# The attention's instructions ordered by a written table, with four queries loaded early and normalisations on two engines

## The chip, the cores and the metric

The kernel runs on one core of a Trainium2 chip. A core has five engines that work side by side, each in the order of its own instruction list: TensorE (PE in the profile; matmuls), VectorE (DVE), ScalarE (ACT), GpSimd (POOL) and SyncE (SP, which here only starts transfers). They wait for each other through semaphores. The metric is the device time of one execution in microseconds (us).

## The reference

A block-summary attention feeds two feed-forward layers of the same form. Each query sees the keys less than 16 positions away and one summary per block of 32 keys (the maximum of the keys, the mean of the values):

```python
k_sum = k.reshape(B, H, nb, block, D).max(axis=3)      # B 2, H 8, S 768, D 64, block 32
v_sum = v.reshape(B, H, nb, block, D).mean(axis=3)
scores_l = scale * q @ k.T                             # kept where |i - j| < 16
scores_s = scale * einsum(q, k_sum) + log(block)
a = softmax(concat(scores_l, scores_s))
x = a @ concat(v, v_sum)                               # 1536 tokens, 512 wide
x = leaky_relu(x @ moe_w_in, 0.01) @ moe_w_out         # 512 -> 2048 -> 512
x = mish(x @ moe2_w_in) @ moe2_w_out
```

The feed-forward weights arrive as 64-bit floats.

## The kernel before

**Groups.** The attention works on 24 groups, each 256 tokens of one batch for one pair of heads; four groups with the same tokens make x for these tokens. A group's steps are: its query transfer (`load_q`, into one of four tiles `qt`, so group g needs that group g-4 has been scored) and its values' transfer (`load_vw`); the key window, copied by GpSimd in two halves (`k_window`, L257: the keys, then the block sums); the scores on TensorE (`scores`, L367); the maximum on VectorE (`score_max`, L381); four exponentials on ScalarE (`score_exp`, L391); the reciprocal of the sum on VectorE (`score_inv`, L400 and L401); the normalisation, one multiplication 128 x 480, on GpSimd (`score_norm`, L406); the transposition on TensorE (`p_transpose`, L412); its evacuation to `pT` on ScalarE or VectorE (`p_evac`, L420 and L422); the product with the values on TensorE (`av`, L431); and x in two parts, the high one as fp32r on ScalarE or VectorE and what is left on VectorE (`x_part`, L446 to L450). Groups 0 to 3 go singly, the others in pairs. Block sums of keys (`k_sum`, L298) and values (`sum_vs`, L340) are made by VectorE, those of the first batch's values by TensorE (`sum_v0`, L317), with an evacuation into the value tiles (`place_v0`, L327 and L329).

**Feed-forward blocks.** A matmul in 32 bits is made of three products of high and low parts. Each step of layer 1 is an up of 12 matmuls per block of tokens (`up`, L465), the activation in two parts (`leaky_a` on ScalarE, L476 and L477; `leaky_b` on VectorE, L481) and a down of 12 matmuls (`down`, L520), which follows three blocks later. Ups and downs are issued in halves of six. Fifteen of them run between the attention's steps; the first six have 256 columns, all others 512.

**Weights.** A weight tile goes through: a transfer into one of three `raw` buffers, the scaling of its top half on ScalarE (`w_scale`, L130), the merge on VectorE (`w_merge`, L137), the high part (`w_hi`, L166 or L164) and the low part on GpSimd (`w_lo`, L173). The tiles of the second part of the weights stand in memory that the attention uses, and can be written once its last step is over.

**Order.** Everything until the attention's end is written as steps with estimated durations, needs, buffers and a turn (partly from the table `RATE`, L64). A planner, `run_order()`, picks the steps one by one on a model of the engines and so sets the order of each engine, of the transfers on SP, and the engine of a step that has two. Where the model finds TensorE idle early on, it puts in matmuls on an idle tile (`warm`, L220). The chosen steps are then issued under a manual schedule. Behind the attention the order is that of the loop over the remaining blocks.

Of the kernel before, what the change touches and what calls it, by code (L numbers as in the profile page):

```python
# [28 lines left out]
def kernel(  # L29
# [182 lines left out]
    def warm(n, w=128):  # L212

        if not idle:
            idle["t"] = ap1.tile([P, 128], F32, name="idle")
            nc.vector.memset(idle["t"], 0.0)
            idle["p"] = bank("h0")
        t = idle["t"]
        for _ in range(n):
            nc.tensor.matmul(idle["p"][:, 0:w], t, t[:, 0:w], start=True, stop=True)  # L220
# [131 lines left out]
    st = {}  # L352

# [71 lines left out]
    def av(g):  # L425

        px, t = st[g]
        w = vw[groups[g][2]]
        for n in range(NB):
            for s in range(2):  # L430
                nc.tensor.matmul(  # L431
                    px[s * D:(s + 1) * D, n * QB:(n + 1) * QB],
                    w[:, n, s, :],
                    t[:, s * (NB // 2) + n // 2, (n % 2) * QB:(n % 2 + 1) * QB],
                    start=True, stop=True,
                )
        st[g] = px
# [137 lines left out]
    if True:  # L575
# [30 lines left out]
        batches = [[g] for g in range(4)] + [[g, g + 1] for g in range(4, NG, 2)]  # L606
        first_score = {g: u for gs, u in zip(batches, (-4, -4, -4, -4) + RATE) for g in gs}
# [4 lines left out]
        steps = []  # L612

        class Step:
            pass

        def step(on, fn, needs=(), turn=0.0, take=(), give=(), tag=None):
            x = Step()
            x.on, x.fn, x.turn, x.take, x.give, x.tag = on, fn, turn, take, give, tag
            x.needs = [(d, 0.07) if isinstance(d, Step) else d for d in needs]  # L620
            x.end = None
            steps.append(x)
            return x

        store = {
            "bank": ["a0", "a1", "y0", "y1", "y2", "y3"], "h": ["h", "h"], "raw": [0] * 3, "top": [0] * 2,
            "mid": [0] * 4, "q": [], "kw": [0] * 4, "s": [0] * 4, "pT": [0] * NPT, "g": [0] * (LAG + 1), "t": [0] * 2,
        }
        held = {}
        closed = [False]  # L630

        def load(fn, mb, needs=(), turn=0.0, take=(), give=()):
            return step({"SP": mb}, fn, needs, turn, take, give)

        def later(f, *a):
            return lambda eng: f(*a)

        def given(x, end):
            x.end = end
            return x  # L640


        landed = [4.1, 5.4, 7.7, 9.0]
        K = {(0, h): given(step({}, None), landed[h]) for h in range(4)}
        Q = {g: given(step({}, None), landed[g] + 0.2) for g in range(4)}
        W_LOAD, W_TOP, W_MERGE, W_HI, W_LO = {}, {}, {}, {}, {}

        def need_slot(i):
            return i if i < 2 * nA else 100

        for i in range(2 * nA):
            u = need_slot(i)
            W_LOAD[i] = load(later(w_load), 0.524, [], max(u - 7, -4.1) if i else -5, [("raw", ("raw", i))])
        for i in range(2 * nA, 2 * nA + 7):
            W_LOAD[i] = load(later(w_load), 0.524, [], 8 + i - 2 * nA, [("raw", ("raw", i))])
# [14 lines left out]
        for h in range(3):  # L670
            PLACE[0, 3].needs.append((PLACE[0, h], -0.4))
# [366 lines left out]
```

## Time and profile before

| what | us |
|---|---|
| time of three runs, median (lowest, highest) | 603.07 (602.11, 603.58) |
| the profiled execution's own time | 602.08 |
| its span, first to last instruction | 599.9 |
| TensorE busy in the span | 589.8 |
| VectorE busy | 384.5 |
| ScalarE busy | 313.9 |
| GpSimd busy | 193.9 |

The time is taken outside the profile; the span is that of the instructions in one profiled execution, and its own time has some 2.2 us around the span. A busy share is a mean over stages of different kind. In the slices of the page TensorE is at 9 tenths or more from the second slice of 15 us to the last but one, and the granted clock of TensorE is 0.999 of full speed over the span.

### The profile page before, as it was taken

To read this page: it belongs to the slowest core of one execution; us is meant where nothing else is said; L and a number is where in the kernel's file an instruction comes from. 1 tells how busy PE (TensorE), PEld (TensorE's weight loads), DVE (VectorE), ACT (ScalarE), POOL (GpSimd) and SP (SyncE) were. 2 spreads that over 40 slices of the span, in tenths; PEclk is the share of its full clock that TensorE was granted. 3 is DMA by queue.
4 is the path that set the end of the run, shared out by engine and by line. 5 is a ranking of instruction groups with operands and counts; after the bars stand their busy time and mean duration, and the time that the engine had idled before them with its cause. 6 is when DMAs were issued, how large, how long until landed. Compare 5 with 4: busy or idle time off the path is not lost.

```text
span 599.9 us, 9152 instructions
## 1 busy us (share of the span) xinstructions
PE 589.8 (98%) x3334; PEld 480.1 (80%) x3334; DVE 384.5 (64%) x777; ACT 313.9 (52%) x671; POOL 193.9 (32%) x214
## 2 busy tenths in 40 slices
PE   8899999999999999999999999999999999999997
PEld 7688878787888888888888888888888888888885
DVE  7799776356451114114445988776799998678684
ACT  5878866357662223225646655454467555444442
POOL 7666742164430001004430323332332232232221
PEclk9999999999999999999999999999999999999999
DMA  9997453026741000001537210000012000001011
GB/s 322 344 311 238 159 167 124 2 87 219 256 140 37 0 2 0 1 0 71 172 109 245 72 35 1 0 1 0 2 70 72 0 1 1 1 35 37 0 72 70
DMA packets 19373, 52.10 MB, mean 87 GB/s; under 512 B 2176, under 2 KB 5248, under 8 KB 19072
## 3 DMA queue, kind: packets, MB, share of 16 engines
q1 hardware_dynamic: 18752, 51.00, 25.6%
q8 instruction: 26, 0.43, 0.3%
q10 hardware_dynamic: 576, 0.52, 0.3%
q14 instruction: 19, 0.16, 0.1%
HBM read 48.37 MB, written 3.15 MB: 86 GB/s over the span
## 4 chain that ended last, share of the span: by engine, by line
PE 94%; DVE 2%; ACT 2%; DMA 1%; POOL 1%; issue 0%; SPq 0%; DVEq 0%; ACTq 0%
PE h L465 43%; PE y L520 22%; PE y L527 21%; PE a L431 2%; PE a L367 2%; PE a L412 1%; PE y L541 1%; DMA kT<-in_kT_dram 1%; DMA raw<-in_moe_w_out_dram 1%; ACT top L130 0%; POOL w L173 0%; DVE s L381 0%; DVE ks L298 0%; DVE mid L137 0%; PE y L317 0%
## 5 line engine op out<-in xcount | busy, mean ns | idle before, releaser
L465 PE MATMUL h<-x,w 128*128 128x512 f32 (+1 forms) x1188 | 288.4, 388 | 0.3 <-ACT g L477 0.2
L465 PEld LDWEIGHTS h<-x,w 128*128 128x128 f32 x1188 | 217.6, 188 | 49.9 <-ACT g L477 0.6
L520 PE MATMUL y<-g,w 128*128 128x512 f32 (+1 forms) x612 | 145.8, 384 | 0.4 <-POOL w L173 0.4
L527 PE MATMUL y<-w,g 128*128 128x512 f32 x552 | 136.9, 394 | 0.0
L194 POOL TENSOR_TENSOR g<-e,g 128x512 fp32r<-128x512 f32 x47 | 73.5, 1565 | 186.7 <-ACT g L191 172.6
L520 PEld LDWEIGHTS y<-g,w 128*128 128x128 f32 x612 | 110.1, 188 | 24.9 <-POOL w L173 0.6
L527 PEld LDWEIGHTS y<-w,g 128*128 128x128 f32 x552 | 103.7, 188 | 24.1
L173 POOL TENSOR_TENSOR w<-mid,w 128x512 fp32r<-128x512 f32 x45 | 63.1, 1410 | 114.4 <-ACT w L166 111.2
L481 DVE TENSOR_TENSOR g<-t,g 128x512 fp32r<-128x512 f32 (+1 forms) x51 | 35.6, 702 | 88.8 <-ACT g L477 88.6
L476 ACT ACTIVATE t<-h 128x512 f32<-128x512 f32 (+1 forms) x51 | 28.9, 567 | 87.1 <-PE h L465 87.1
L137 DVE SCALAR_TENSOR_TENSOR mid<-raw,top 128x512 int32<-128x512 int32 x64 | 56.7, 894 | 26.6 <-POOL w L173 15.1
L130 ACT ACTIVATE top<-raw 128x512 f16<-128x512 bf16 x64 | 50.2, 797 | 26.5 <-DMA raw<-in_moe_w_out_dram 8.9
L492 ACT ACTIVATE e<-h 128x512 f32<-128x512 f32 x48 | 28.7, 598 | 67.6 <-PE h L465 60.0
L503 DVE SCALAR_TENSOR_TENSOR u<-u,r 128x512 f32<-128x512 f32 x48 | 37.1, 773 | 25.8 <-ACT r L496 25.5
L495 ACT ACTIVATE r<-u,two 128x512 f32<-128x512 f32 x48 | 34.8, 724 | 31.0 <-DVE u L494 31.0
L391 ACT ACTIVATE s<-s,nm 128x120 f32<-128x120 f32 x96 | 36.5, 382 | 14.8 <-DVE nm L381 14.6
L166 ACT CAST w<-mid 128x512 fp32r<-128x512 f32 x62 | 37.7, 617 | 11.5 <-DVE mid L137 6.8
L191 ACT CAST g<-e 128x512 fp32r<-128x512 f32 x48 | 29.5, 615 | 20.6 <-DVE e L505 20.5
L494 DVE SCALAR_TENSOR_TENSOR u<-e 128x512 f32<-128x512 f32 x48 | 34.6, 720 | 1.1
L406 POOL TENSOR_TENSOR s<-s,r 128x480 f32<-128x480 f32 x24 | 24.7, 1032 | 30.1 <-DVE r L401 25.8
L504 DVE SCALAR_TENSOR_TENSOR u<-u,r 128x512 f32<-128x512 f32 x48 | 33.2, 691 | 1.4
L505 DVE SCALAR_TENSOR_TENSOR e<-e,u 128x512 f32<-128x512 f32 x48 | 33.1, 689 | 1.1
(71 smaller groups left out, 432.9 us busy)
## 6 DMA issues: line engine op xcount, KB each, us to landing
raw<-in_moe_w_in_dram SPq DMA_DIRECT2D x32, 512.0 KB, 4.3
raw<-in_moe_w_out_dram SPq DMA_DIRECT2D x32, 512.0 KB, 3.8
vw<-in_vW_dram SPq DMA_DIRECT2D x24, 192.0 KB, 5.2
kT<-in_kT_dram SPq DMA_DIRECT2D x8, 400.0 KB, 7.3
out_dram<-yp SPq DMA_DIRECT2D x12, 256.0 KB, 2.0
q<-in_qT_dram SPq DMA_DIRECT2D x20, 128.0 KB, 7.1
vS<-in_vS_dram SPq DMA_DIRECT2D x2, 1024.0 KB, 8.8
v<-in_v_dram SPq DMA_DIRECT2D x2, 768.0 KB, 7.9
```

What stands on the lines that cost most here:

```text
L130: (tc.keep_in_program_order if pin else id)(nc.scalar.mul(out=do, in_=di, mul=4.0))
L137: nc.vector.scalar_tensor_tensor(out=d, in0=wraw.pop(i)[:, 0:2 * DM].rearrange("p (f w) -> p f w", w=2)[:, :, 1], scalar=13, in1=wtop.pop( ...
L166: nc.scalar.copy(out=w[:, 0], in_=wmid[i])
L173: (eng or nc.gpsimd).tensor_sub(out=w[:, 1], in0=wmid.pop(i), in1=w[:, 0].bitcast(F32))
L194: (nc.vector if lo == "dve" else nc.gpsimd).tensor_sub(out=dst_lo, in0=src, in1=dst_hi.bitcast(F32))
L391: nc.scalar.activation(out=s[:, n], in_=s[:, n], func=AF.Exp, scale=-1.0, bias=nm[:, n:n + 1], accum_out=sm[:, n:n + 1],)
L465: nc.tensor.matmul(ph[:, 0:n], w[:, a, kt * P:(kt + 1) * P], x[:, c, kt, o:o + n], start=(kt == 0 and i == 0), stop=(kt == KT - 1 and i == 2),
L481: nc.vector.tensor_sub(out=g[:, 1, 0:n], in0=t[:, 0:n], in1=g[:, 0, 0:n].bitcast(F32))
L495: nc.scalar.activation(out=r, in_=u, func=AF.Ln, bias=two[:, 0:1])
L503: V.scalar_tensor_tensor(out=u, in0=u, scalar=2.0, in1=r, op0=ALU.add, op1=ALU.mult)
L520: mm = nc.tensor.matmul(y[d][:, o:o + n], w[:, a, d * P:(d + 1) * P], g[:, c, 0:n], start=sta and not second, stop=sto,)
L527: nc.tensor.matmul(y[d], g[:, a, d * P:(d + 1) * P], w[:, c], start=sta, stop=sto,)
```

## The change

The planner, its steps, `RATE` and the estimates go. In their place stands `ORDER`, a text of words, each one step: a letter for the kind, the group's or block's number, a letter for the engine where there is a choice (a, d, p for ScalarE, VectorE, GpSimd) and, behind a colon, the PSUM banks. V, v, w, q, k, r are transfers (first batch's values, windows of values, weights, queries, second batch's keys and values); K and J key sums; C and D the two parts of a key window; S, M, E, I, N, T, P, A the group's steps from scores to the product with the values; X and L the parts of x; t, m, h, l the steps of a weight; s, p the value sums of the first batch and their placement, R, Z those of the second; U, O halves of an up or a down; G, g the two parts of its activation; d the evacuation of y; warm the idle matmuls. The words are issued one after another.

Three things besides are new. The queries of groups 4 to 7 go to a tile of their own, `early`, in the memory that x's second block takes later. `score_norm` has an engine: 11 of the 24 normalisations are VectorE's, 13 GpSimd's. `leaky_b` has one as well: 12 of the first 15 blocks' subtractions are GpSimd's, six of 256 columns and six of 512. By the letters some more steps change their engine: three evacuations of `pT` and four high parts of x go from VectorE to ScalarE, three high parts of weights, two low parts and one placement to VectorE. There are 29 idle matmuls instead of 23.

```diff
-    RATE = (-1.0, -0.5, 3.5, 4.0, 6.5, 7.0, 7.0, 9.5, 10.5, 13.0)
+    ORDER = """
+        V.0 K.0 C.0 v.1 D.0 w.0 K.1 C.1 S.0:a0,a1 V.1 D.1 M.0 warm.1 S.1:y0,y1 q.5 E.0 C.2 q.6 M.1 w.1 E.1 C.3 I.0
+        v.0 K.2 C.4 N.0d C.5 I.1 warm.11 T.0:a0 D.4 v.3 K.3 D.2 N.1p S.2:a1,y0 q.4 P.0a D.3 M.2 C.6 S.3:y1,y2 E.2
...
+    """
...
+    SINGLE = 4
...
+    early = xp.tile([P, 2 * KT * TB], F32, tag="x1", name="early")
+    qe = [early[:, i * GT:(i + 1) * GT].rearrange("p (t n) -> p t n", n=NB) for i in range(4)]
+
     def load_q(g, eng):
         b, c, hp = groups[g]
-        t = qt[g % len(qt)]
+        t = qe[g - 4] if 4 <= g < 8 else qt[g % len(qt)]
...
-    def score_norm(g):
+    def score_norm(g, eng):
         s, r = st[g]
-        nc.gpsimd.tensor_mul(out=s, in0=s, in1=r.unsqueeze(2).to_broadcast([P, NB, WN]))
+        ENG[eng].tensor_mul(out=s, in0=s, in1=r.unsqueeze(2).to_broadcast([P, NB, WN]))
...
-    def leaky_b(t, g, n):
-        nc.vector.tensor_sub(out=g[:, 1, 0:n], in0=t[:, 0:n], in1=g[:, 0, 0:n].bitcast(F32))
+    def leaky_b(t, g, n, eng=None):
+        (eng or nc.vector).tensor_sub(out=g[:, 1, 0:n], in0=t[:, 0:n], in1=g[:, 0, 0:n].bitcast(F32))
         return g
...
+        def step(name, fn, *a):
+            run[name] = lambda eng, banks: fn(*a, *([eng] if eng else []), *([banks] if banks else []))
...
+            for word in ORDER.split():
+                name, _, banks = word.partition(":")
+                eng = engines.get(name[-1])
+                name = name.rstrip("adp") if eng else name
+                if name.startswith("warm"):
+                    warm(int(name[5:]))
+                else:
+                    run[name](eng, banks.split(",") if banks else None)
```

What the table does to the lists is shown at three places. The first is GpSimd's list at the start, before, from the second half of group 1's window to the second normalisation (`kw<-kT` is a copy of keys, `kw<-ks` of block sums, `s<-s,r` a normalisation):

```order
L257 TENSOR_SCALAR kw<-ks 128x4x24
L257 TENSOR_SCALAR kw<-kT_110 128x4x64
L257 TENSOR_SCALAR kw<-kT_110 128x4x32
L257 TENSOR_SCALAR kw<-kT_110 128x4x64
L257 TENSOR_SCALAR kw<-kT_110 128x4x32
L257 TENSOR_SCALAR kw<-ks 128x4x24
L406 TENSOR_TENSOR s<-s,r 128x480
L257 TENSOR_SCALAR kw<-ks 128x4x24
L406 TENSOR_TENSOR s<-s,r 128x480
```

The same stretch in the changed kernel, whose lines are 30 to 31 higher:

```order
L287 TENSOR_SCALAR kw<-ks 128x4x24
L287 TENSOR_SCALAR kw<-kT_111 128x4x64
L287 TENSOR_SCALAR kw<-kT_111 128x4x32
L287 TENSOR_SCALAR kw<-kT_111 128x4x64
L287 TENSOR_SCALAR kw<-kT_111 128x4x32
L287 TENSOR_SCALAR kw<-kT_111 128x4x64
L287 TENSOR_SCALAR kw<-kT_111 128x4x32
L287 TENSOR_SCALAR kw<-kT_111 128x4x64
L287 TENSOR_SCALAR kw<-kT_111 128x4x32
L287 TENSOR_SCALAR kw<-ks 128x4x24 x2
L437 TENSOR_TENSOR s<-s,r 128x480
L287 TENSOR_SCALAR kw<-ks 128x4x24
```

Two further groups' key windows and one more pair of block sums now stand ahead of the second normalisation, and the first one has left this list.

The second place is VectorE's list from the reciprocal of group 2 on, before (`mid<-raw,top` is a weight's merge, `vw<-y` a placement, `pT<-y` an evacuation, `x` the first high part):

```order
L400 TENSOR_SCALAR r<-sm 128x4
L401 RECIPROCAL r<-r 128x4
L137 SCALAR_TENSOR_TENSOR mid<-raw,top_86 128x512
L400 TENSOR_SCALAR r<-sm 128x4
L401 RECIPROCAL r<-r 128x4
L327 COPY vw_99<-y_309 24x512
L422 COPY pT<-y_366 120x512
L450 CAST x_401<-a_269 128x256
```

The changed kernel from the same reciprocal on:

```order
L431 TENSOR_SCALAR r<-sm 128x4
L432 RECIPROCAL r<-r 128x4
L437 TENSOR_TENSOR s<-s,r 128x480
L164 SCALAR_TENSOR_TENSOR mid<-raw,top_86 128x512
L191 CAST w<-mid 128x512
L357 COPY vw_100<-a_324 24x512
L431 TENSOR_SCALAR r<-sm 128x4
L432 RECIPROCAL r<-r 128x4
L357 COPY vw_101<-a_324 24x512
L453 COPY pT<-y_374 120x512
L164 SCALAR_TENSOR_TENSOR mid<-raw,top_87 128x512
```

The normalisation of group 2 and the high part of the first weight are now in this list, two placements instead of one, and the reciprocal of group 3 stands between them.

The third is TensorE's list around the last product with the values (`a<-pT,vw`), before; `h<-x,w` is an up, `y<-g,w` a down:

```order
L412 MATMUL a_1893<-ident,s 120x128 x4
L465 MATMUL h<-x_1012,w 128x512 x6
L465 MATMUL h<-x_1606,w 128x512 x5
L520 MATMUL y_1666<-g,w 128x512
L431 MATMUL a_1878<-pT,vw_100 64x64 x8
L431 MATMUL a_1893<-pT,vw_101 64x64 x8
L465 MATMUL h<-x_1606,w 128x512 x6
L520 MATMUL y_1666<-g,w 128x512 x2
```

The changed kernel:

```order
L443 MATMUL a_1898<-ident,s 120x128 x4
L496 MATMUL h<-x_1054,w 128x512 x6
L496 MATMUL h<-x_1649,w 128x512 x4
L462 MATMUL a_1893<-pT,vw_100 64x64 x8
L462 MATMUL a_1898<-pT,vw_101 64x64 x8
L496 MATMUL h<-x_1649,w 128x512 x6
L551 MATMUL y_1547<-g,w 128x512
```

In all, 282 matmuls of 512 columns (two of 256 counted as one) stand ahead of the last product, where it was 271; the downs behind it are taken in thinner slices. The next up that waits before, the 12 matmuls at 145.61 below, stands 89 such matmuls behind the product, and 86 in the changed kernel.

## Rows read from the trace of the kernel before

**Rows 1.** Busy time by stretch: us from:to, length, PE, PEld, DVE, ACT, POOL, clock, DMA, GB/s

```profile
0.00:40.00 40.00, 33.76 (x468) 29.09 (x472) 31.64 (x118) 28.36 (x96) 27.64 (x69) 1.00 0.99 327
29.00:52.00 23.00, 21.38 (x279) 19.63 (x279) 21.29 (x71) 17.90 (x64) 15.09 (x25) 1.00 1.00 305
40.00:500.00 460.00, 459.74 (x2459) 372.82 (x2452) 279.44 (x546) 243.91 (x509) 140.46 (x130) 1.00 0.24 78
```

**Rows 2.** Timeline of TensorE, first 45 us: start, us, instruction, count, idle before

```profile
7.59 2.50 PE L220 MATMUL h<-idle 128*128 128x128 f32 x20
10.14 0.75 PE L367 MATMUL y<-kw,q 64*64 64x120 f32 x16
...
21.44 0.50 PE L367 MATMUL a<-kw,q 64*64 64x120 f32 x4 [0.41 <-DMA q<-in_qT_dram]
...
30.81 1.15 PE L431 MATMUL a<-pT,vw 120*64 120x64 f32 x32 [1.11 <-DVE pT L422]
...
40.34 1.70 PE L520 MATMUL y<-g,w 128*128 128x256 f32 x12
```

**Rows 3.** Timeline of GpSimd, first 45 us

```profile
8.62 0.67 POOL L257 TENSOR_SCALAR kw<-kT 128x256 f32<-128x256 f32 x2 [0.69 <-DMA kT<-in_kT_dram]
9.81 0.27 POOL L257 TENSOR_SCALAR kw<-ks 128x96 f32<-128x96 f32 x1 [0.53 <-DVE ks L298]
10.05 0.99 POOL L406 TENSOR_TENSOR s<-s,r 128x480 f32<-128x480 f32 x1
...
13.94 1.27 POOL L406 TENSOR_TENSOR s<-s,r 128x480 f32<-128x480 f32 x1
...
35.74 1.28 POOL L173 TENSOR_TENSOR w<-mid,w 128x512 fp32r<-128x512 f32 x1 [1.42 <-ACT w L166]
```

**Rows 4.** Timeline of ScalarE, first 45 us

```profile
13.00 0.38 ACT L391 ACTIVATE s<-s,nm 128x120 f32<-128x120 f32 x1
...
15.62 0.57 ACT L329 COPY vw<-y 24x512 f32<-24x512 f32 x1
...
23.78 0.39 ACT L391 ACTIVATE s<-s,nm 128x120 f32<-128x120 f32 x1
...
30.05 0.56 ACT L420 COPY pT<-a 120x512 f32<-120x512 f32 x1
```

**Rows 5.** Timeline of VectorE, first 45 us

```profile
13.71 0.66 DVE L137 SCALAR_TENSOR_TENSOR mid<-raw,top 128x512 int32<-128x512 int32 x1
...
16.23 0.69 DVE L327 COPY vw<-y 24x512 f32<-24x512 f32 x1 [0.77 <-ACT vw L329]
```

**Rows 6.** ScalarE's groups by line and shape, 0 to 60 us: busy, mean ns, idle

```profile
L130 ACT ACTIVATE top<-raw 128x512 f16<-128x512 bf16 x11 | 8.7, 795 | 2.7 <-DMA raw<-in_moe_w_in_dram 2.1 <-DMA raw<-in_moe_w_out_dram 0.5
L166 ACT CAST w<-mid 128x512 fp32r<-128x512 f32 x7 | 4.4, 628 | 0.8 <-DVE mid L137 0.8
L420 ACT COPY pT<-a 120x512 f32<-120x512 f32 x6 | 3.3, 581 | 1.3 <-PE a L412 1.3
...
L448 ACT CAST x<-a 128x256 fp32r<-128x256 f32 x4 | 1.5, 373 | 0.2 <-PE a L431 0.2
```

**Rows 7.** VectorE's groups by line and shape, the whole span

```profile
L340 DVE TENSOR_REDUCE vs<-vS 128x16 f32<-128x512 f32 x8 | 8.4, 1050 | 0.0
L298 DVE TENSOR_REDUCE ks<-kT 128x24 f32<-128x768 f32 x8 | 7.5, 938 | 0.9 <-DMA kT<-in_kT_dram 0.9
L422 DVE COPY pT<-a 120x512 f32<-120x512 f32 x11 | 7.4, 687 | 6.2 <-PE a L412 6.1
...
L164 DVE CAST w<-mid 128x512 fp32r<-128x512 f32 x2 | 0.8, 411 | 0.0
```

**Rows 8.** Timeline of TensorE and VectorE at the attention's end

```profile
123.35 1.15 PE L431 MATMUL a<-pT,vw 120*64 120x64 f32 x32
...
145.61 3.07 PE L465 MATMUL h<-x,w 128*128 128x512 f32 x12 [0.17 <-ACT g L477]
...
127.16 5.18 DVE L137 SCALAR_TENSOR_TENSOR mid<-raw,top 128x512 int32<-128x512 int32 x3 [1.19 <-POOL w L173]
```

More of the change, by code (lines that the diff above doesn't have):

```diff
@@ L219, in warm @@
         for _ in range(n):
[L220 removed]
+            nc.tensor.matmul(idle["p"][:, 0:P], t, t, start=True, stop=True)
     def build_const():
@@ L423, in p_evac, with av @@
         st[g] = (pp, t)
[L425 to L437, printed above, removed]
+    def av(gs):
+        for g in gs:
+            px, t = st[g]
+            w = vw[groups[g][2]]
+            for n in range(NB):
+                for s in range(2):
+                    nc.tensor.matmul(
+                        px[s * D:(s + 1) * D, n * QB:(n + 1) * QB],
+                        w[:, n, s, :],
+                        t[:, s * (NB // 2) + n // 2, (n % 2) * QB:(n % 2 + 1) * QB],
+                        start=True, stop=True,
+                    )
+            st[g] = px
     def x_part(g, c, eng):
@@ L605 @@
         NI = len(items)
-        batches = [[g] for g in range(4)] + [[g, g + 1] for g in range(4, NG, 2)]
-        first_score = {g: u for gs, u in zip(batches, (-4, -4, -4, -4) + RATE) for g in gs}
+        batches = [[g] for g in range(SINGLE)] + [[g, g + 1] for g in range(SINGLE, NG, 2)]
         X = 15
[L612 to L640, printed above, removed]
@@ L643 @@
[L643 to L655, printed above, removed]
@@ new lines @@
+        run = {}
+        def step(name, fn, *a):
+            run[name] = lambda eng, banks: fn(*a, *([eng] if eng else []), *([banks] if banks else []))
+        for i in range(2 * nA + 7):
+            step(f"w.{i}", w_load)
+        for i in range(2 * nA + 4):
+            step(f"t.{i}", w_scale)
+            step(f"m.{i}", w_merge, False)
+            step(f"h.{i}", w_hi)
+            step(f"l.{i}", lambda eng: w_lo(ENG[eng]))
+        for i in range(2):
+            step(f"V.{i}", load_v0, i, SP)
+            step(f"s.{i}", sum_v0, i)
+            step(f"r.{i}", load_vs, i, SP)
+            for q in range(4):
+                step(f"R.{4 * i + q}", sum_vs, i, q)
@@ new lines @@
+        for h in range(4):
+            step(f"K.{h}", k_sum, 0, h)
+            step(f"k.{h}", load_k, 1, h, SP)
+            step(f"J.{h}", k_sum, 1, h)
+            step(f"p.{h}", place_v0, h)
+            step(f"Z.{h}", place_vs, h)
+        for g in range(NG):
+            step(f"q.{g}", load_q, g, SP)
+            step(f"v.{g}", load_vw, g, SP)
+            step(f"C.{g}", k_window, g, 0)
+            step(f"D.{g}", k_window, g, 1)
+            step(f"M.{g}", score_max, g)
+            step(f"E.{g}", score_exp, g)
+            step(f"I.{g}", score_inv, g)
+            step(f"N.{g}", score_norm, g)
+            step(f"T.{g}", p_transpose, g)
+            step(f"P.{g}", p_evac, g)
+            step(f"X.{g}", x_part, g, 0)
+            step(f"L.{g}", x_part, g, 1, None)
@@ new lines, with up_half, act_a, act_b @@
+        for gs in batches:
+            step(f"S.{gs[0]}", scores, gs)
+            step(f"A.{gs[0]}", av, gs)
+        def up_half(n, half):
+            _, _, _, j, o, N, _, sidx, _ = slots[n]
+            if half == 0:
+                gq[n] = up_begin(n)
+            up(sidx, j, o, N, gq[n], half)
+        def act_a(n):
+            gq[n] = leaky_a(gq[n], slots[n][5])
+        def act_b(n, eng):
+            gq[n] = leaky_b(*gq[n], slots[n][5], ENG[eng])
+        def down_half(m, half):
+            nonlocal cur_y
+            _, layer, _, _, o, N, i, sidx, last = slots[m]
+            if i == 0 and o == 0 and half == 0:
+                cur_y = new_y()
+            down(sidx, layer, i == 0, last, o, N, gq[m], cur_y, half)
+            if half == 1:
+                gq.pop(m)
@@ new lines, in drain_half @@
+        def drain_half(j, eng):
+            drain(0, 0, j, 0, TB, cur_y, eng)
+        for n in range(X):
+            step(f"G.{n}", act_a, n)
+            step(f"g.{n}", act_b, n)
+            for half in range(2):
+                step(f"U.{2 * n + half}", up_half, n, half)
+                step(f"O.{2 * n + half}", down_half, n, half)
+        for j in range(2):
+            step(f"d.{2 * j}", drain_half, j, "act")
+            step(f"d.{2 * j + 1}", drain_half, j, "dve")
+        engines = {"a": "act", "d": "dve", "p": "pool"}
```

295 lines of the change are left out of this document (30 added, 265 removed).

## The prediction, made before the changed kernel was run

> **What bounds the kernel now.** I read the busy time by stretches first, then TensorE's timeline where the stretches show gaps, then the other engines' timelines at those gaps. From 40 to 500 us TensorE is busy 459.74 of 460.00 [rows 1]: no order of the same matmuls gains there. In the first 40 us it is busy 33.76, so 6.25 are idle, and some of the busy time is filler: 46 records of .125 each, the first 20 of them 2.50 [rows 2], 5.75 us. So 12 us at the start is all that an order can win, and it is won only if the chain that feeds TensorE gets shorter: a group's scores, maximum, exponentials, normalisation, transposition, evacuation and product with the values. Here the other engines are the limit: VectorE is busy 21.29 of 23.00 from 29 to 52 us [rows 1]. So the question is how far TensorE's useful work is ahead at 40 us, and whether the lead lasts to the end.
>
> Words below: S, M, E, I, N, T, P, A of a group are those eight steps in turn (I is the reciprocal); X and L are the high and low part of its x; C and D the two halves of a key window; t, m, h, l the four steps of a weight (scaling, merge, high part, low part); U and O half an up or a down of a block.
>
> **The start, to the placement of the value sums.** The letters for engines and the new order work together here. Up to 9.29, when GpSimd has copied the second key window (8.62 + .67, [rows 3]), both kernels do the same. Before, GpSimd goes on to group 2's window sums at 9.81 (.27), and TensorE scores group 2 at 10.14 [rows 2, 3]. In the changed kernel GpSimd copies groups 4 and 5 first (C.4, C.5: 2 x .67) and two sums (D.4, D.2: 2 x .27): 9.29 + 1.34 + .54 = 11.17, so S.2 at 11.2, 1.05 later. What covers this is that ScalarE and GpSimd lose other work from the chain: N.0 and N.2 go to VectorE, and the scaling of the first weight comes behind E.2 instead of ahead of it. From S.2 to the end of E.2 it was 10.14 to 13.00, 2.86 [rows 2, 4]; so E.2 ends at 14.06. Then P.1 .58, t.0 .80 [rows 6], m.0 .68 (.66 in [rows 5], and a handoff), h.0 .41 on VectorE [rows 7]: 16.55 with the handoffs, where the first placement can begin; before it began at 15.62 [rows 4].
>
> N on VectorE is in no row. Its bounds: 480 of 512 columns of the .66 of an undisturbed merge [rows 5], .62, and the 1.73 that a merge took beside GpSimd's subtractions (5.18 for three, [rows 8]). I take .65, since GpSimd at the start mostly copies; at the upper end it is the third rival. Low parts of g on GpSimd aren't there either: half of a 512-wide subtraction's 1.28 [rows 3], .64, up to a normalisation's .99. I take .66. VectorE takes over 11 N, 7.2 us, and gives up 12 of 51 low parts of g (six of 256 columns, six of 512: at N's .65 for 480 columns, 6.2) and three P (2.1); the rest that changes hands is a few high parts either way. Its sum is the same within 2 us; what changes is when it works.
>
> **The placements and the first up.** Four placements run one after another in both kernels, VectorE's .69, ScalarE's .57 [rows 4, 5]: 2 x .69 + 2 x .57 + handoffs = 2.65, so 19.2. Behind them, each waiting for the one before or standing behind it in ScalarE's row, P.2 on VectorE .69, m.1 .68, h.1 .63, P.3 .58, A.3 .69 (16 matmuls, from the timeline's 32 in 1.15, [rows 2], and the drain), X.3 .37 [rows 6, 7]: 3.64, and with the handoffs E.4 begins at 23.0. Before it began at 23.78 [rows 4]. This is the **early queries'** share: before, S.4 waited .41 for its query until 21.44 [rows 2], since each of the four query tiles is free only when group g-4 has been scored. Four more queries in x's memory need no such wait; S.4 then hangs on its windows and banks, which are there by 20. The gain is not .41 but what E.4 can use, .8 with the shorter work ahead of it on ScalarE. The four loads cost SP nothing new (20 + 0 before, 16 + 4 now), but they stand ahead of two weight loads; no weight is wanted so early that this shows (the second is scaled at about 17).
>
> **From E.4 to 40 us.** E.4 to E.7 are back to back on ScalarE, 23.78 to 30.05 [rows 4], 6.27, and will be again: 29.27. I.7 .4 and P.5 .69 [rows 7], then A.4 at 30.5; before 30.81 [rows 2]. The up behind it waits for GpSimd, which has N.7 .99 and a low part 1.28 [rows 3] ahead: 32.2, against 31.9 before. VectorE's two value sums (1.05 each, [rows 7]), P.7 and the scores of 8 bring A.6 to 33.7 and S.8 to 36.3; key sum J.3 .94 [rows 7], a merge and L.7 bring the second half of up 3 to 37.55, and 4 ups in all are done at 39.1 with half an up more; two downs then end at 40.55. Before, at 40.34, TensorE has done U.0 to U.7, O.0, O.1 and the same scores [rows 2]. The changed kernel at 40.55 has U.8 too, which is worth .77 (half of 12 matmuls of 256, 1.70 less the overlap, [rows 2]). **Lead: .77 - .21 = .6 us.**
>
> **From 40 us on.** The two lists of TensorE hold the same matmuls, and TensorE in both is full as long as every operand is early enough. In the changed order VectorE is back to back from 29 to 52, and hands A.8 its operand at 52.0 to 52.35 when TensorE is about to ask at the same time; I put it at nothing, the margin being some tenths. The attention's end moves: the last A stands 11 matmuls of 512 columns later in TensorE's work. Behind it the weights of the next part start (their memory is the attention's), and before, TensorE ran from 123.35 to 145.44 on work that didn't need them, then waited .17 [rows 8]. Less A's own 1.08 that is 89 matmuls of .236 average; now it is 86, 21.4 us of cover instead of 22.1. If the weight chain keeps its 22.26, the stall is .87, .7 more. But drains and merges stand earlier in the new order, so the chain may shorten by as much. Bounds: -.17 (stall gone) to +.7; I take 0, since in the new order the drains of y stand behind two merges of that chain on VectorE, where four stood ahead of them, and the chain's last wait before was ScalarE's g behind a weight's scaling, which the order now sets otherwise.
>
> **The sum.** The profiled execution took 602.08 (span 599.92 and 2.16 around it); the median of the three runs shown is 603.07, .99 above. The forecast goes on the median: 603.07 - .6 = **602.5**, and by bounds of the end alone 601.7 to 603.2. The handoffs, some thirty of .05 to .1, make it 601.3 to 603.7.
>
> **Rivals.**
> *No lead, 603.1.* Two engines in each other's way: GpSimd's normalisation beside a merge on VectorE took 1.27 at 13.94 and .99 alone at 10.05 [rows 3, 5]. If N.0 on VectorE and C.5 on GpSimd can't run together, C.5, D.2, S.2 and all behind start .63 later, and the .6 is gone. For: that row. Against: GpSimd's row there is a normalisation with two inputs, and the window copies at the start, with one, show no such lengthening (.67 beside VectorE's key sums). The Trainium skill, "SBUF — State Buffer", section "Who interferes with whom", says that a VectorE instruction with two SBUF inputs contends with a GpSimd instruction that reads SBUF, and that whoever issues first holds the shared pair for the whole instruction while the other is fully blocked; by it N.0 holds C.5 up for all of its .65, which speaks against this change. The trace agrees in part: a full block would have cost that normalisation .43 (from 13.94 to the merge's end at 14.37), and it lost .28.
>
> *More lead, 600.8.* By my dates TensorE still has gaps of 3.4 us between 20 and 40 us (the largest before U.4, .95, and before S.8, .65). Several hang on handoffs that I put too long or on an engine's order that leaves room. If half closes, 1.7 more. For: the early queries let every later score be moved freely. Against: VectorE's list has no free place in it.
>
> *Slower, 605.6: VectorE is the bound from 29 to 52 us.* It has in the changed order hardly a pause there (before, 1.71 of 23 us [rows 1]). If the three merges m.3 to m.5 meet GpSimd's low parts of g and take 1.73 each [rows 8] instead of .68, everything behind on VectorE is 3.15 later, A.8 with it, and TensorE waits. The price decides from 2.4 us: .6 of lead and 1.8 to be seen. For: low parts on GpSimd, eleven N on VectorE, both inputs of each in the memory they share. Against: at 13.71 [rows 5] it was GpSimd that lost time and the merge took .66.
>
> **How the numbers follow.** Chances: forecast .45, more lead .25, no lead .13, slower .17. A measurement of this kernel tells some 0.3% from no change, 1.8 us: faster is under 601.3, slower above 604.9. The faster case lies below 601.3 with .22 of its .25, the forecast's own lower edge adds .08: faster .30. Slower: .15 of the third rival and .01 of the forecast's upper edge, .16. The same: .54. The range has to take in most of more lead and the lower part of slower: 600.2 to 604.9 leaves out about .07 below and .13 above.
>
> **What would show it.** In the changed profile: S.2 on TensorE at 11.2 and E.4 on ScalarE at 23.0 (start right); A.4 at 30.5 and two downs ended at 40.55 with half an up more (lead right); N on VectorE at .62 to .70 (or above 1: a rival); TensorE from 42 to 120 without a gap above .2; the wait behind the last A under .9. It is wrong if the first 40 us hold much less filler and idle time than 11.4, or if VectorE is late at A.8.

## The result, and the profile of the changed kernel

The changed kernel takes **607.23 us** (median of 14 runs, 603.55 to 611.47), the kernel before, run beside it, 602.62. The ratio is 1.0074, with a 95% interval of 1.0049 to 1.0099: slower by 4.6 us, outside the range of 600.2 to 604.9. One of the 14 runs of the kernel before took 3293.85 us; without it its median is 602.51. The profiled execution happens to be the longest of the 14: 611.47, with a span of 609.7, 9.8 more than before.

Busy time by stretch, with the columns of [rows 1]; two of its stretches come first:

```profile
0.00:40.00 40.00, 35.65 (x478) 30.64 (x479) 31.66 (x116) 26.64 (x93) 27.39 (x69) 0.96 1.00 317
40.00:500.00 460.00, 453.95 (x2413) 367.26 (x2413) 277.05 (x535) 242.43 (x506) 138.24 (x126) 0.99 0.25 79
10.00:20.00 10.00, 8.47 (x110) 6.26 (x108) 6.95 (x29) 5.94 (x23) 6.64 (x17) 0.83 1.06 328
89.00:98.00 9.00, 8.60 (x61) 6.33 (x65) 4.67 (x25) 5.73 (x22) 3.06 (x7) 0.63 0.12 36
```

From 40 to 500 us TensorE is idle 6.05 us, where it was idle .26 before. And the granted clock, 1.00 in the same stretches before, is .83 from 10 to 20 us and .63 from 89 to 98: in these stretches TensorE stood partly at the lower of its two levels, 1.2 of 2.4 GHz. Where that is, TensorE's timeline shows (start, us, instruction, count, and in brackets idle time and what ended it):

```profile
12.06 0.38 PE L398 MATMUL a<-kw,q 64*64 64x120 f32 x2 [0.54 <-POOL kw L287]
...
41.74 2.32 PE L496 MATMUL h<-x,w 128*128 128x256 f32 x18
...
50.47 1.06 PE L443 MATMUL a<-ident,s 128*120 128x128 f32 x8 [0.80 <-DVE nm L412]
...
65.57 1.23 PE L398 MATMUL a<-kw,q 64*64 64x120 f32 x32 [0.97 <-PE h L496]
...
89.40 2.50 PE L496 MATMUL h<-x,w 128*128 128x512 f32 x5 [3.83 <-DVE x L477]
91.83 1.89 PE L398 MATMUL a<-kw,q 64*64 64x120 f32 x32
93.65 3.96 PE L496 MATMUL h<-x,w 128*128 128x512 f32 x12
...
135.56 1.15 PE L462 MATMUL a<-pT,vw 120*64 120x64 f32 x32
```

The accounts, taken at the last product with the values, since the work behind it comes out .2 us apart in the two profiles. Before it stood at 123.35 [rows 8]; 11 matmuls of .236 more stand ahead of it now, so 125.9 would be level, and 135.56 is 9.6 late. These are:
- .6 at 40 us: the two half downs (O.0 and O.1, "two downs" in the prediction) end at 41.74, where before that work was done at 41.11 (40.34 [rows 2] and .77 for the half up more);
- 2.2 in four waits from 40 to 80 us, the largest at 50.47 and 65.57;
- 3.83 in one wait at 89.40, for x;
- 2.8 behind that wait, at the lower clock: the five matmuls take 2.50 instead of some 1.3, the next scores 1.89 instead of 1.23 (at 65.57), the up 3.96 instead of 3.07 [rows 8].

That is 9.4; .2 stay open. So 6.6 of the 9.6 hang on the one wait at 89.40, in this longest of the 14 executions; one near the median follows in the experiments. ScalarE's timeline there:

```profile
24.77 0.40 ACT L422 ACTIVATE s<-s,nm 128x120 f32<-128x120 f32 x1
...
83.06 0.79 ACT L157 ACTIVATE top<-raw 128x512 f16<-128x512 bf16 x1 [2.58 <-DMA raw<-in_moe_w_out_dram]
83.72 0.35 ACT L479 CAST x<-a 128x256 fp32r<-128x256 f32 x1
87.56 0.77 ACT L157 ACTIVATE top<-raw 128x512 f16<-128x512 bf16 x1 [3.50 <-DMA raw<-in_moe_w_in_dram]
88.21 0.34 ACT L479 CAST x<-a 128x256 fp32r<-128x256 f32 x1
```

L157 is the scaling of a weight, L479 the high part of x. The second scaling waits 3.50 us for its transfer, and the high part X.15 stands behind it in ScalarE's list, with the up of TensorE behind X.15 and L.15. ScalarE's list of the changed kernel shows the same without a run (`top<-raw` is a scaling, `x<-a` a high part of x, `yp<-y` an evacuation of y):

```
L157 ACTIVATE top_87<-raw 128x512
L479 CAST x_1054<-a_1370 128x256
L157 ACTIVATE top_86<-raw 128x512
L479 CAST x_1054<-a_1378 128x256
L588 ACTIVATE yp<-y_782 128x512
L588 ACTIVATE yp<-y_784 128x512
```

The first scaling is t.15, which the table puts ahead of X.14. The second is t.16, the 17th weight's, and **the table has no such word**: the loop behind the attention issues it, in the code long behind X.15. It reached its place when the kernel was built. Below it is moved.

### The profile page after: what moved, and what is told of

Read it like the earlier page. It is cut to its first block, busy times and chain, and to the rows that moved or that the text cites. A ratio compares the mean times of both kernels' runs of the same rounds, so it can differ in the third digit from the quotient of the medians.

```text
span 609.7 us, 9107 instructions
## 1 busy us (share of the span) xinstructions
PE 595.2 (98%) x3346; PEld 483.6 (79%) x3346; DVE 389.7 (64%) x775; ACT 315.6 (52%) x674; POOL 194.4 (32%) x213
## 4 chain that ended last, share of the span: by engine, by line
PE 91%; DMA 4%; DVE 3%; POOL 1%; issue 1%; ACT 0%; SPq 0%; ACTq 0%; POOLq 0%
PE h L496 43%; PE y L558 21%; PE y L551 21%; DMA vS<-in_vS_dram 2%; PE a L462 1%; PE a L398 1%; DMA raw<-in_moe_w_in_dram 1%; PE a L443 1%; DMA kT<-in_kT_dram 1%; PE y L572 1%; DVE vs L370 1%; POOL kw L287 1%; DVE s L412 0%; PE a L347 0%; PE y L398 0%
## 5 line engine op out<-in xcount | busy, mean ns | idle before, releaser
L551 PE MATMUL y<-g,w 128*128 128x512 f32 (+1 forms) x612 | 144.0, 383 | 0.0
L200 POOL TENSOR_TENSOR w<-mid,w 128x512 fp32r<-128x512 f32 x43 | 60.0, 1407 | 96.5 <-ACT w L193 91.1
L512 DVE TENSOR_TENSOR g<-t,g 128x512 fp32r<-128x512 f32 x39 | 32.1, 825 | 84.4 <-ACT g L508 84.2
L157 ACT ACTIVATE top<-raw 128x512 f16<-128x512 bf16 x64 | 50.4, 798 | 28.0 <-DMA raw<-in_moe_w_in_dram 10.5
L526 ACT ACTIVATE r<-u,two 128x512 f32<-128x512 f32 x48 | 34.8, 724 | 30.5 <-DVE u L525 30.5
L193 ACT CAST w<-mid 128x512 fp32r<-128x512 f32 x59 | 35.5, 617 | 11.6 <-DVE mid L164 5.5
L528 DVE TENSOR_TENSOR e<-u,h 128x512 f32<-128x512 f32 x48 | 32.8, 684 | 1.1
```

Source lines behind the costliest of these rows:

```text
L157: (tc.keep_in_program_order if pin else id)(nc.scalar.mul(out=do, in_=di, mul=4.0))
L193: nc.scalar.copy(out=w[:, 0], in_=wmid[i])
L200: (eng or nc.gpsimd).tensor_sub(out=w[:, 1], in0=wmid.pop(i), in1=w[:, 0].bitcast(F32))
L526: nc.scalar.activation(out=r, in_=u, func=AF.Ln, bias=two[:, 0:1])
L551: mm = nc.tensor.matmul(y[d][:, o:o + n], w[:, a, d * P:(d + 1) * P], g[:, c, 0:n], start=sta and not second, stop=sto,)
```

## The experiments

In the short diffs of `ORDER` a changed row is cut to the words around the change. With each median stands in round brackets that of the kernel before, run beside it, and then the ratio with its 95% interval. The ratio is not formed from the two medians and can differ from theirs by a tenth of a per cent. The runs again, t16, t16_noearly and t16_norm were on one chip, before_t14, t16_r4, t16_g6 and t16_r4_g6 on a second, drain and drain_warm on a third; across chips only the distances from the kernel before can be compared.

**again: the changed kernel once more.**

> The changed kernel once more, for a second profile. In the first one TensorE waits 3.83 us at 85.56 for a part of x that stands behind a weight's scaling on ScalarE, and its clock is granted at half for some us after that and at 14 to 18 us. Theory 'scaling in front of x': the wait is there again, 2 to 4 us, since it follows from the order and from when one weight transfer lands; time 605 to 608. Rival 'a bad execution': no such wait, time within 1 us of the kernel before plus the gaps of VectorE (1 to 2 us).

607.9 us (602.54), 1.0082 [1.0055, 1.0109]. In this profile (span 606.5) the granted clock at the start is 1.00, and the wait is there again, with slow matmuls behind it. TensorE's timeline:

```profile
86.09 1.49 PE L496 MATMUL h<-x,w 128*128 128x512 f32 x5 [2.01 <-DVE x L477]
87.51 1.89 PE L398 MATMUL a<-kw,q 64*64 64x120 f32 x32
89.33 3.71 PE L496 MATMUL h<-x,w 128*128 128x512 f32 x12
```

2.01 of wait, .2 + .66 + .64 for the clock: 3.5 us in an execution near the median. The fallen clock at the start belongs to some executions, the stall to the order.

**t16: one instruction moved.** The scaling t.16 becomes a word of the table, behind the two drains of y, where the kernel before has it.

```diff
-        d.0 U.19 S.16:a0,a1
+        d.0 t.16 U.19 S.16:a0,a1
...
+        step(f"t.{2 * nA + 4}", w_scale)
...
-                        w_scale(layer == 0 and order[items[cnt["scale"]][0]][1] == 1)
+                        if cnt["scale"] == cnt["merge"]:
+                            w_scale(layer == 0 and order[items[cnt["scale"]][0]][1] == 1)
```

> One instruction moved: the scaling of the seventeenth weight (the first that belongs to the loop behind the attention) goes behind the two drains of y on ScalarE, where the kernel before has it, instead of ahead of the last high part of x of the second block. Theory 'scaling in front of x': the wait of 3.83 us at 85.56 is under 0.3, and so is the clock's fall behind it; the time falls by 3.5 to 5 us, to 602.5 to 604. Rival 'VectorE is late throughout': the next wait takes its place and the time stays above 605.

603.88 us (602.54), 1.0022 [1.0005, 1.0038]: 4.0 less than the changed kernel on the same chip. ScalarE's timeline:

```profile
23.41 0.39 ACT L422 ACTIVATE s<-s,nm 128x120 f32<-128x120 f32 x1
...
80.60 0.61 ACT L479 CAST x<-a 128x256 fp32r<-128x256 f32 x2
...
83.90 0.79 ACT L157 ACTIVATE top<-raw 128x512 f16<-128x512 bf16 x1 [1.69 <-DMA raw<-in_moe_w_in_dram]
```

Both high parts of x run in one go, and the scaling waits 1.69 for its transfer with nothing urgent behind it. TensorE's timeline of the same kernel:

```profile
11.93 0.38 PE L398 MATMUL a<-kw,q 64*64 64x120 f32 x2 [0.55 <-POOL kw L287]
...
30.83 1.15 PE L462 MATMUL a<-pT,vw 120*64 120x64 f32 x32
...
40.49 2.32 PE L496 MATMUL h<-x,w 128*128 128x256 f32 x18
...
48.64 1.06 PE L443 MATMUL a<-ident,s 128*120 128x128 f32 x8 [0.36 <-DVE nm L412]
...
63.73 1.23 PE L398 MATMUL a<-kw,q 64*64 64x120 f32 x32 [0.97 <-PE h L496]
...
81.92 2.96 PE L496 MATMUL h<-x,w 128*128 128x512 f32 x12
...
126.99 1.15 PE L462 MATMUL a<-pT,vw 120*64 120x64 f32 x32
...
176.96 2.37 PE L551 MATMUL y<-g,w 128*128 128x512 f32 x9 [0.51 <-DVE yp L590]
```

The up at 81.92 waits for nothing. The two half downs are done at 40.49, .6 ahead of 41.11; but the last product stands at 126.99, 1.1 behind 125.9. So the lead is there at 40 us and is lost by 65, in the waits at 48.64 and 63.73 and some smaller ones. What is late there is on VectorE:

```profile
45.92 1.08 DVE L370 TENSOR_REDUCE vs<-vS 128x16 f32<-128x512 f32 x1 [1.24 <-DMA vS<-in_vS_dram]
...
58.80 1.75 DVE L164 SCALAR_TENSOR_TENSOR mid<-raw,top 128x512 int32<-128x512 int32 x1
...
61.59 1.70 DVE L512 TENSOR_TENSOR g<-t,g 128x512 fp32r<-128x512 f32 x1
63.21 0.41 DVE L477 TENSOR_TENSOR x<-a,x 128x256 fp32r<-128x256 f32 x1
```

GpSimd's subtraction beside that merge:

```profile
58.35 1.65 POOL L200 TENSOR_TENSOR w<-mid,w 128x512 fp32r<-128x512 f32 x1 [2.23 <-DVE w L191]
```

The value sum R.4 stands ahead of its transfer's landing and waits 1.24, with the maxima behind it for which T.8 on TensorE waits. And a merge and a low part of g (g.6) take 1.75 and 1.70 instead of .68, ahead of L.10, the low part of x at 63.21. The row of the scores at 63.73 gives TensorE's own up as its releaser, but that was long done; L.10 and L.11 free the banks that these scores write, and they come last.

**t16_noearly: t16 without the early queries.** The queries of groups 4 to 7 go to the four old tiles again, behind S.3.

```diff
-        t = qe[g - 4] if 4 <= g < 8 else qt[g % len(qt)]
+        t = qt[g % len(qt)]
```

> As t16, without the tile for early queries: queries 4 to 7 go to the four tiles once groups 0 to 3 are scored, and queries 9 and 10 are loaded behind query 8. If the early queries are worth what I put on them, scores 4 come .4 to .8 later and the time is up to 0.8 above t16. If they are hidden, no difference above 0.3.

603.66 us (602.54), 1.0015 [1.0001, 1.003]: .2 less than t16, with intervals that overlap. TensorE's timeline, at S.4:

```profile
21.76 1.24 PE L398 MATMUL y<-kw,q 64*64 64x120 f32 x32 [1.37 <-DMA q<-in_qT_dram]
...
41.31 2.32 PE L496 MATMUL h<-x,w 128*128 128x256 f32 x18
...
125.97 1.15 PE L462 MATMUL a<-pT,vw 120*64 120x64 f32 x32
```

So S.4 does wait for its query, 1.37, and runs 1.1 later than in t16 (20.66). E.4 is .9 later (24.35 against 23.41) and the two half downs end .8 later, at 41.31, .2 behind the kernel before: in t16 the early queries make the lead at 40 us. Yet t16_noearly then has no wait above .1 up to the last product, which stands at 125.97, 1.0 earlier than in t16: R.4 waits only .35 for its transfer there, and g.6 takes .68. What the early queries win by 40 us, t16 gives back in its waits, and the time shows nothing of it.

**t16_norm: t16 with all 24 normalisations on GpSimd.**

```diff
-        v.0 K.2 C.4 N.0d C.5 I.1
+        v.0 K.2 C.4 N.0p C.5 I.1
```

(and the other ten N likewise).

> As t16, and all 24 normalisations on GpSimd. If VectorE's eleven normalisations are what makes its list late, this is faster than t16 by 1 to 2 us (waits of .8 at 50 us and 1.0 at 65 us gone). If they pay, as I took it, it is slower by 0.5 to 2, most of it at the start, where GpSimd copies key windows. If the first normalisation collides with the window copies, the second scores start earlier than the 12.06 of the changed kernel's profile in spite of the fuller GpSimd.

604.43 us (602.54), 1.0029 [1.0013, 1.0045]: .55 more than t16; the intervals overlap, so that the gain of the second engine is not settled. GpSimd's timeline at the start, of t16_norm and then of t16:

```profile
8.61 1.30 POOL L287 TENSOR_SCALAR kw<-kT 128x256 f32<-128x256 f32 x4 [0.69 <-DMA kT<-in_kT_dram]
9.87 0.99 POOL L437 TENSOR_TENSOR s<-s,r 128x480 f32<-128x480 f32 x1
10.82 0.67 POOL L287 TENSOR_SCALAR kw<-kT 128x256 f32<-128x256 f32 x2
```

```profile
9.07 2.33 POOL L287 TENSOR_SCALAR kw<-kT 128x256 f32<-128x256 f32 x6 [0.69 <-DMA kT<-in_kT_dram]
```

The same six copies (C.5 the last two) take 1.30 + .67 = 1.97 without a normalisation on VectorE and 2.33 with N.0 beside them (9.86 to 10.61), 2.39 in again: N.0 does hold C.5 up, by .36 to .42. In exchange GpSimd is spared the .99. S.2 is at 12.01 instead of 11.93, although the keys of t16_norm landed .46 earlier; at equal landings it would be some .5 later. That S.2 comes ahead of 12.06, the sign I had named for a collision, is due to this landing and says nothing; the copies' own lengths do. Two things more are in this profile. The two half downs end at 40.72, in spite of the earlier keys .2 behind t16, so the normalisations on VectorE do pay at the start. And S.12 still waits, .98 at 63.17: VectorE's normalisations aren't what makes it late there.

**before_t14: the stall put into the kernel before.** The scaling of the 15th weight, with its load, is put just ahead of X.15 in the planner's list; all else is the kernel before.

```diff
+            seq = run_order()
+            seq.remove(W_TOP[14])
+            seq.insert(seq.index(XH[15]), W_TOP[14])
+            seq.remove(W_LOAD[14])
+            seq.insert(seq.index(W_TOP[14]), W_LOAD[14])
```

> The kernel before, with the scaling of its fifteenth weight (whose transfer lands at 81.6 in its profile) put ahead of the second half of the high parts of x of the second block on ScalarE, which it runs at 76.7. Theory 'scaling in front of x': ScalarE waits for the transfer, x's part comes near 82.5 instead of 77, TensorE waits 3 to 4 us for the banks and for x at 79 to 84, and its clock is granted at half for some us behind; 606 to 609 in place of 602.5. Rival 'the wait costs only in the changed kernel, because VectorE is late there': under 1 us.

606.56 us (603.11), 1.0049 [1.0032, 1.0067]. ScalarE's timeline, and then TensorE's:

```profile
82.96 0.77 ACT L130 ACTIVATE top<-raw 128x512 f16<-128x512 bf16 x1 [5.56 <-DMA raw<-in_moe_w_in_dram]
83.61 0.34 ACT L448 CAST x<-a 128x256 fp32r<-128x256 f32 x1
```

```profile
84.46 1.88 PE L367 MATMUL a<-kw,q 64*64 64x120 f32 x28 [4.06 <-DVE x L446]
86.27 3.70 PE L465 MATMUL h<-x,w 128*128 128x512 f32 x12
```

The same three lines as in the changed kernel: a scaling that waits for its transfer, X.15 behind it, TensorE 4.06 idle and then a first up at 3.70 (this profiled execution is the longest of the four). Nothing else of the change is needed for it. The cost is 3.45 us by the medians, 1.9 to 4.0 by the interval.

**t16_r4, t16_g6, t16_r4_g6: the two late places on VectorE.** In the first R.4 goes behind M.11 and stands next to R.5; in the second g.6 goes behind L.10; the third has both.

```diff
-        U.10 M.9 l.5p U.11 E.9 I.8 S.10:a0,a1 J.2 C.12 N.8p O.2 G.4 q.14 R.4 q.15 D.12 O.3
-        N.9p O.5 E.10 M.11 g.5p O.6 R.5 C.13
+        U.10 M.9 l.5p U.11 E.9 I.8 S.10:a0,a1 J.2 C.12 N.8p O.2 G.4 q.14 q.15 D.12 O.3
+        N.9p O.5 E.10 M.11 g.5p O.6 R.4 R.5 C.13
...
-        U.15 g.6d Z.2 L.10 l.9p t.10 S.12:a0,a1
+        U.15 Z.2 L.10 g.6d l.9p t.10 S.12:a0,a1
```

> As t16, and the fifth value sum of the second batch goes behind the maxima of groups 9 to 11 on VectorE, as in the kernel before. In t16 it holds VectorE 1.24 us at 45.9 until a transfer has landed. If that is what makes VectorE late, the waits of TensorE at 48.6 (.36) and at 63.7 (.97) go and the time falls by .8 to 1.3, to 602.6 to 603.1. If the transfer is late in any place, or the second wait has a cause of its own, it falls by under .5.

603.75 us (603.11), 1.0006 [.999, 1.0023], with a spread of 5.4 us. That is .6 over the kernel before, where t16 was 1.3 over; the intervals overlap, so that the fall of .8 to 1.3 is neither shown nor ruled out. T.8 no longer waits; S.12 still does, .97, so its wait has a cause of its own. In its profile the clock fell at the start (columns as above):

```profile
10.00:20.00 10.00, 7.99 (x98) 5.74 (x96) 5.81 (x26) 5.16 (x21) 7.02 (x18) 0.66 1.05 343
```

> As t16, and one subtraction of g on VectorE, which took 1.70 us at 61.6 beside a subtraction of a weight's low part on GpSimd, goes behind the low part of x that frees the scores' banks. If the lengthened instruction is what makes the scores of groups 12 and 13 wait .97 at 63.7, that wait goes and the time falls by about 1, to 602.9. If VectorE is late there in any case, a wait of .4 or more stays.

603.59 us (603.11), 1.0008 [.9992, 1.0024]. S.12 comes without a wait, at 61.38, as the theory has it. The time is .5 over the kernel before, and again the interval overlaps that of t16.

> As t16, with both moves. If the two waits are what TensorE lost after 40 us, the lead at 40 us of .6 stays to the end of the attention, and the time is 602.0 to 602.6, the kernel before within 0.1%. If other waits take their place, 603 or more.

602.99 us (603.11), 1.0004 [.9992, 1.0016]: no difference from before that can be told, as forecast for the case that the two waits are what was lost; t16 was 1.3 over. Both waits are gone and the last product stands at 124.93, 1.0 ahead of level. Not all of it is the two moves: the keys landed early in this execution (8.48 against 9.07 in t16), and the two half downs are done at 39.61, a lead of 1.5, of which .5 is lost up to the last product; t16 loses 1.7 there. The 1.0 is given back 50 us later. TensorE's timeline, and then VectorE's:

```profile
39.61 2.32 PE L496 MATMUL h<-x,w 128*128 128x256 f32 x18
...
124.93 1.15 PE L462 MATMUL a<-pT,vw 120*64 120x64 f32 x32
...
175.92 2.37 PE L551 MATMUL y<-g,w 128*128 128x512 f32 x9 [1.76 <-DVE yp L590]
```

```profile
170.10 1.77 DVE L164 SCALAR_TENSOR_TENSOR mid<-raw,top 128x512 int32<-128x512 int32 x1 [1.18 <-POOL w L200]
171.80 3.47 DVE L512 TENSOR_TENSOR g<-t,g 128x512 fp32r<-128x512 f32 x2
175.19 1.28 DVE L590 TENSOR_SCALAR yp<-y 128x512 f32<-128x512 f32 x2
```

The down at 175.92 writes y's banks again and needs them drained; VectorE's half of the drain comes at 175.19, behind a merge and two low parts of g that take 1.77 and 3.47 instead of .68 and 1.37, since GpSimd runs low parts of weights (L200) at the same time. The weights of that stretch are written into the attention's memory. TensorE came earlier, the drain did not: in t16_noearly, t16_g6 and t16_r4_g6 the last product stands at 125.97, 125.41 and 124.93, and the down that waits begins at 176.03, 175.97 and 175.92. What sets the date of the chain ahead of this drain, no run here shows.

**drain, drain_warm: that wait, and the start.** On top of t16_r4_g6, `drain` puts all four evacuations of the third block's y on ScalarE; `drain_warm` adds three idle matmuls, two ahead of S.2 and one ahead of S.3.

```diff
-                if d % 2 == 0:
+                if d % 2 == 0 or (layer == 0 and j == 2):
```

```diff
-        T.0:a0 D.4 v.3 K.3 D.2 N.1p S.2:a1,y0 q.4
+        T.0:a0 warm.2 D.4 v.3 K.3 D.2 N.1p S.2:a1,y0 warm.1 q.4
```

> The last one with all four evacuations of y of the third block on ScalarE, two of which were on VectorE. There they stood at 175.2 behind a merge and two subtractions of g that took 1.7 us each beside GpSimd's low parts of weights, and TensorE waited 1.76 for the bank at 175.9. If the lead that was won ahead of the attention's end is given back at that wait, the wait goes and the time falls by 1.2 to 1.8, to 601.2 to 601.8, under the kernel before. If the next wait of the weight chain behind the attention takes it, it falls by under .4.

602.84 us (602.68), 1.0013 [.9998, 1.0028]. The wait of 1.76 is gone: from the last product to the end it takes 474.5 (601.1 - 126.59), in t16_r4_g6 it was 476.3 (601.2 - 124.93). But in this execution the last product came 1.7 later, and the fall of 1.2 to 1.8 isn't in the time: drain can't be told from the kernel before, as t16_r4_g6 could not be.

> As the one before, with three more idle matmuls, two ahead of the scores of group 2 and one ahead of those of group 3, where TensorE idles .3 to 1.2 and .4 us. In two profiles TensorE's clock was granted at .66 and .83 of full speed over 10 to 20 us behind these pauses, and the first product with the values came 1.5 to 3 us later. If the pauses are what lets it fall, no run is more than 1.5 us above the median and the median falls by up to .5; if not, the spread stays as it is and the idle matmuls cost up to .3.

**601.67 us** (602.68), 0.9979 [0.9966, 0.9991]: 1.0 faster than the kernel before, the only one of these that is. Its 12 runs lie within 2.1 us (600.86 to 602.92), those of drain within 4.5. Busy time from 10 to 20 us:

```profile
10.00:20.00 10.00, 8.71 (x147) 7.12 (x147) 8.45 (x31) 7.44 (x25) 6.76 (x15) 1.00 1.05 342
```

The two kernels differ in three idle matmuls only; they fill pauses of TensorE ahead of S.2 and S.3 that were .54 and .44 in drain's profile. No run is more than 1.3 above the median, as forecast for the case that the pauses matter, but the median falls by 1.2, where I had said up to .5. So what the three matmuls change is not settled; the last section comes back to it.

## Why the prediction was wrong, step by step

**The step that failed is "From 40 us on"**, with its words "I put it at nothing" and, in the list of what would show it, TensorE without a gap above .2. It rested on TensorE's matmuls being the same and on VectorE's dates at A.8, the only operand that it followed behind 40 us. It did not ask what stands ahead of x's high parts on ScalarE. There a weight's scaling that waits for a transfer had come ahead of X.15, by 2.0 to 3.8 us of wait and 1.5 to 2.8 of lower clock behind it. This is shown from both sides: moved away it gives back 4.0 us (t16), put into the kernel before, with another weight's scaling, it costs 3.45 (before_t14). The list of ScalarE, which stands before any run, has it; the prediction rests on places in the lists of GpSimd, VectorE and TensorE, and on none in ScalarE's.

**The rivals.** None named this, so the chance of .17 for slower stood for another cause. The slower one had VectorE as the bound and merges at 1.73. That mechanism exists: 1.75 and 1.70 at 58.80 and 61.59 in t16. But it is two instructions, not three at another place, and its price is the .97 of S.12, a wait that goes when g.6 is moved (t16_g6). The Trainium skill, "SBUF — State Buffer", section "Who interferes with whom", says that a VectorE instruction with two inputs in SBUF contends with a GpSimd instruction that reads SBUF, and that the ports they share are held exclusively. The trace agrees but for .13: if the merge had stood still until GpSimd's subtraction beside it was done (58.35 + 1.65 = 60.00), it would have ended .68 later, and it ended .55 later, at 60.55. *No lead* named a mechanism that is there, at .36 to .42 instead of .63 (t16_norm): the copies with one input, which the prediction held against it, do lengthen beside a normalisation. But the lead at 40 us is there with it: E.4 doesn't pass on all that S.2 is late. *More lead* was not seen in the time, though the profiles of t16_g6 and t16_r4_g6 have 1.5 at 40 us.

**The start: the mechanism right, the size partly by luck.** In t16, where the clock stayed up and the order until there is the same, S.2 is at 11.93 (forecast 11.2), E.4 at 23.41 (23.0), A.4 at 30.83 (30.5), the two half downs end at 40.49 (40.55). Of the .7 at S.2 .45 is the landing of the keys (9.07 against 8.62 [rows 3]) and .36 the longer C.5. So the lead of .6 at 40 us came out although the dates on the way were .3 to .7 late: from A.4 on it took 9.66 where the forecast had 10.05. And with the keys at 8.48, near the 8.62 that the forecast assumed, the lead is 1.5 (half downs at 39.63 in t16_g6, 39.61 in t16_r4_g6), not .6. In the profile of the changed kernel itself E.4 is at 24.77 and the lead is -.6, with the clock at .83 from 10 to 20 us.

**The early queries: right up to 40 us.** I had given them the .8 at E.4. S.4 came 1.1 us earlier by them, E.4 .9 and the half downs .8 (t16 against t16_noearly). The time didn't fall, since t16 loses that lead again behind 40 us.

**The prices.** Groups of the changed kernel by line and shape (busy, mean ns, idle), VectorE's and then GpSimd's:

```profile
L437 DVE TENSOR_TENSOR s<-s,r 128x480 f32<-128x480 f32 x11 | 7.6, 689 | 0.3
```

```profile
L512 POOL TENSOR_TENSOR g<-t,g 128x512 fp32r<-128x512 f32 x6 | 8.2, 1362 | 16.8 <-ACT g L508 15.4 <-issue 1.4
L512 POOL TENSOR_TENSOR g<-t,g 128x256 fp32r<-128x256 f32 x6 | 4.9, 823 | 3.2 <-ACT g L508 3.0 <-POOL kw L287 0.2
```

A normalisation on VectorE takes .69 where I took .65 within .62 to 1.73; the low part of 256 columns on GpSimd .82, where I took .66 within .64 to .99. But that VectorE's sum stays the same within 2 us was wrong: it is busy 389.7 us in the changed kernel and 389.8 in t16, 384.5 before, 5.3 more. The 11 normalisations cost 7.6, while its low parts of g fall only from 35.6 to 32.1, less than the 6.2 that I subtracted: the 39 that stay take .82 each instead of .74.

**The lead after 40 us.** It would not have lasted without the stall either: t16 has it at 40.49 and is 1.1 late at the last product. The "some tenths" of margin that I gave VectorE at A.8 were less than none at R.4, whose transfer had not landed, and at g.6.

**The attention's end.** Bounds -.17 to +.7, taken at 0. The wait that the term speaks of came out so: an up waits .19 for ScalarE's g in t16, .17 before. What the term leaves out is a second wait 30 us later, for the drain: .51 in t16, and 1.76 with the lead kept (t16_r4_g6). The term was bounded as a fixed cover, but this drain keeps its date while the last product moves by 1.0 (125.97 to 124.93), so what TensorE gains ahead of it comes back as wait. One slip besides: by these bounds the forecast lies in 602.3 to 603.2, not from 601.7 on.

**The sum.** Again is 5.4 us over the kernel before beside it, and 4.0 of these are the scaling (again against t16). What is left is 1.3 by the medians of t16 and before, and 2.3 by their two profiled spans (602.2 and 599.9): 1.1 at the last product, .5 in the waits behind it (.70 against .17), and .7 that the runs don't attribute. The forecast had -.6 for all of that.

## What to carry to other kernels

In a list that an engine works in order, look at each instruction that waits for a transfer, and ask what behind it the bounding engine needs; compare these places in the list of every engine, ScalarE's too, before trusting a sum made from busy times. Code that stands behind a hand-written order can be built into it: put its first instructions into the table where their place matters. A lead won at the start is kept only if the next date that doesn't depend on it, here a landing and a drain, moves as well. And before a date at the start is credited to the order, the landing that it hangs on has to be compared too.

## What was not expected of the hardware

**The clock behind a stall.** Each of the three profiles with the stall has TensorE at the lower level behind it: waits of 3.83, 2.01 and 4.06 us, and then an up of 3.96, 3.71 and 3.70 instead of 2.96 to 3.07. The wait of 1.76 in t16_r4_g6 had no such sequel (12 matmuls of a down in 2.91 at 180.00). So in these three a stall of 2.0 to 4.1 us cost 1.4 to 2.8 more than it lasted.

**The clock at the start.** In two profiles, of the changed kernel and of t16_r4, the clock from 10 to 20 us was .83 and .66, behind pauses of .3 to 1.2 us; in again and t16, with pauses much the same, it was 1.00 (in again one of 1.19, in t16_r4 one of 1.18). What decides stays open. In t16_r4 it goes with the time: the five runs with a mean clock of .997 or less took 604.3 to 606.3, the four with 1.000 took 600.9 to 602.5. But it isn't all of the spread: the longest runs of t16 (607.67) and t16_g6 (606.52) and three of drain (604.0 to 605.2) have 1.000. Another thing that differs from one profile to the next is the landing of the keys, 8.47 to 9.71, and the half downs follow it. Three more idle matmuls went with a spread of 2.1 instead of 4.5 us and a median 1.2 lower; that the clock is the reason, no profile shows, since both profiled executions had it at 1.00, and in the two profiles the keys landed at 9.07 (drain) and 8.47 (drain_warm).
